# Making masks, triangle and scales on chip instead of loading them, in a gated linear attention followed by a maxout network

## The chip, the core and the metric

The kernel runs on one core of a Trainium2 chip. A core has five engines with a queue of their own each: PE (TensorE, matrix products; its weight loads are shown as PEld), DVE (VectorE), ACT (ScalarE), POOL (GpSimd) and SP (SyncE, which here issues all transfers). Each engine works through its instructions strictly in program order, and waits on semaphores where an instruction needs a result of another engine or of a transfer. The metric is the time of one execution on the device in microseconds; lower is better. The kernel before took 141.66 us (median of three runs, 141.11 to 141.95).

## What is computed

```python
for t in range(S):                       # q, k, v, alpha: (4, 8, 768, 48)
    state = alpha[:, :, t, :, None] * state + np.einsum('bhd,bhe->bhde', k[:, :, t], v[:, :, t])
    y[:, :, t] = np.einsum('bhd,bhde->bhe', q[:, :, t], state)
x = y.transpose(0, 2, 1, 3).reshape(B * S, H * D)          # (3072, 384)
h = np.maximum(np.maximum(x @ w1, x @ w2), x @ w3)         # w1, w2, w3: (384, 768)
out = h @ w_out                                            # w_out: (768, 384)
```

Inputs and output are float32; inside, most products are of float16 operands.

## The kernel before

The recurrence is done in 12 steps. Step s handles 256 tokens of batch s mod 4, so steps 0 to 3 are the first third of the sequence of the four batches, and a step needs the state that step s - 4 left. The 256 tokens are two units of 128 tokens, and within a unit two neighbouring tokens share a partition (R = 2). For each step four loads of 384 KB bring alpha, q, k and v (`load`, one letter of "akqv" for the tile: ra, rk, rq, rv) into rings of four buffers, as rows of 384 bytes.

Then, for a step: alpha of a pair is multiplied (`pair_decay`, m), its logarithm taken (`logs`, N, `inverse`, r), and PE sums the logarithms along the sequence with a triangular matrix `upto` and a 4-column matrix `pick` (`sums`, c). Exponentials of these sums are the decays (`decay_in` e, `decay_out` f, `totals` g), by which DVE or POOL scale k and q (`near_k` u, `near_q` w, `scale_k` k, `scale_q` q). v is scaled by a column constant `vs_c` (V). PE turns q and k with the identity `ident` (T, kept by t), or, from step 5 on, a transfer turns them (D). PE forms the scores (A, line L304), DVE multiplies them by the causal mask `pmask`, or by `rowmask`, spread from it, for step 0 (`masked`, a), PE applies them to v and applies q to the state (Y, L330), and the result is kept as xT (x). The new state is formed by S, s, z and y, with gates M.

The network uses max(a, b, c) = a + max(0, b - a, c - a) with the maximum kept in hT: `differ` (d, L418) makes w2 - w1 and w3 - w1 as `wdif`; the w1 part goes straight to the output as x (w1 w_out), a product that is formed once from a halved w1 (`halve` b, turned by B, kept by n) and w_out (C, P, p). For each step six gate products G of six matmuls (L452) are reduced by `maxed` (h), and two or more output products O (L486) of nine matmuls are scaled by `ys_c` (o) and stored (W). Weight tiles K0 to K8 are column blocks of w1, w2, w3 (K3 is block 1 of w1), K9 to K11 pairs of row blocks of w_out. K0 to K7 are first loaded into the ring buffers that steps 2 and 3 will use for alpha, q, k and v, so for instance `l0@2` (alpha of step 2) can be issued only when K0 has been read by d0, d1 and b0.

The order of everything is a string, `ORDER`. A piece such as `k0v@1` is: letter, index, engine (v DVE, p POOL, a ACT), step; `#` names the PSUM banks. Nothing reorders it: each engine gets its pieces in this order. `H` pieces are warm matmuls on a zeroed tile, which compute nothing; `H2^k0@1` also waits for a named piece. Before the order, `clear_padding` zeroes padding columns: DVE the 16 half states and two la tiles, POOL the vu, qk and vt tiles.

The constants `upto`, `pick`, `vs_c`, `ys_c`, `undo_c` come as one array `ca` (34.5 KB), and `ident` and `pmask` as `cb` (64 KB), both computed on the host, and loaded by the pieces J1 and J0 between the first loads:

```python
        l0@0 J1@0 l1@0 J0@0 l3@0 l0@1 r0a@0 m0v@0 l2@0 N0a@0 r1a@0 u0v@0 H15@0#0 c0@0#0 g0a@0 e0a@0 K0@0 f0a@0
```

Of the kernel before, what the change touches and what calls it, by code (L numbers as in the profile page):

```python
# [10 lines left out]
FP16 = mybir.dt.float16  # L11

# [11 lines left out]
def kernel(  # L24
# [39 lines left out]
    rr = np.arange(P)  # L64
    tri_np = (
        ((rr[:, None] > MID) & (rr[:, None] <= rr[None, :])).astype(np.float16)
        - ((rr[:, None] <= MID) & (rr[:, None] > rr[None, :])).astype(np.float16)
    )
    w2_np = np.stack([rr <= MID, rr > MID], 1).astype(np.float16)
    ur, jr = rr // J, rr % J  # L70
    same = (ur[:, None] == ur[None, :]).astype(np.float16)
    upto_np = same * np.tile(tri_np[R - 1::R, R - 1::R], (U, U))
    pick_np = np.zeros((P, U, 2), np.float16)
    for u in range(U):
        pick_np[u * J:(u + 1) * J, u] = w2_np[::R]
    token = np.concatenate([R * np.arange(J) + r for r in range(R)])
    pmask_np = (token[:, None] <= token[None, :]).astype(np.float16)
    at_pair = LAM * (R * jr + R - 1 - MID)
    at_token = LAM * (rr // R * R + R - 1 - MID)
    c32_np = np.stack(  # L80
        [np.exp(at_pair + SIGMA), np.exp(-at_token - SIGMA), 0 * rr - LAM * P / 2], 1
    ).astype(np.float32)
    ca_np = np.concatenate([np.concatenate([upto_np, pick_np.reshape(P, -1)], 1).view(np.float32), c32_np], 1)
    cb_np = np.concatenate([np.eye(P, dtype=np.float16), pmask_np], 1)

# [28 lines left out]
    def load_weight(_, i, eng):  # L114
        home = staged(i)
        if i < 9:
            w = (moe_w1, moe_w2, moe_w3)[i % 3]
            queues[eng].dma_start(home.rearrange("p (f j) -> p f j", f=NF),
                                  w.rearrange("(f p) j -> p f j", p=P)[:, :, i // 3 * 2 * P:(i // 3 + 1) * 2 * P])
        else:  # L120
            queues[eng].dma_start(home.rearrange("p (j m) -> p j m", j=2),
                                  moe_w_out.rearrange("(j p) m -> p j m", p=P)[:, 2 * (i - 9):2 * (i - 8)])

    ca = cpool.tile([P, P // 2 + U + 3], FP32, name="ca")
    cb = cpool.tile([P, 2 * P], FP16, name="cb")
    rowmask = cpool.tile([P, R, P], FP16, name="rowmask")

    def load_const(_, i, eng):
        c, c_np = ((ca, ca_np), (cb, cb_np))[i]
        queues[eng].dma_start(c, nc.inline_tensor(c_np, name=f"c{i}").ap())  # L130

    half = ca.bitcast(FP16)
    upto, pick = half[:, :P], half[:, P:P + 2 * U]
    c32 = ca[:, P // 2 + U:]
    ident, pmask = cb[:, :P], cb[:, P:2 * P]
    vs_c, ys_c, undo_c = c32[:, 0:1], c32[:, 1:2], c32[:, 2:3]
# [6 lines left out]
    sts = [[cpool.tile([P, HP, 2, D], FP16, name=f"st{b}_{i}") for i in range(2)] for b in range(B)]  # L143

    def clear_padding():
        for st in (st for pair in sts for st in pair):
            for i in range(2):
                nc.vector.memset(st[64 * i:64 * (i + 1), :, 1 - i], 0.0)
        for la in las:
            nc.vector.memset(la.rearrange("p r a b c -> p (r a b) c")[:, :, D:], 0.0)  # L150
        for vu in vus:
            nc.gpsimd.memset(vu.rearrange("p u a b c -> p (u a b) c")[:, :, D:], 0.0)
        for qk, vt in zip(qks, vts):
            nc.gpsimd.memset(qk.rearrange("p r i a b c -> p (r i a b) c")[:, :, D:], 0.0)
            nc.gpsimd.memset(vt.rearrange("p a b c -> p (a b) c")[:, :, D:], 0.0)


# [69 lines left out]
    def sums(s, *_):  # L227
# [4 lines left out]
        for p in range(HP):  # L232
            for n, (r, _) in enumerate(parts):
                nc.tensor.matmul(lps(s, 1)[:, H * D + 2 * U * p:H * D + 2 * U * (p + 1)],
                                 las[s % 2][:, r, p].rearrange("p a b -> p (a b)"), pick,
# [71 lines left out]
    def spread_mask(_, i, eng):  # L307
        for u in range(U):
            for r in range(R):
                copy(eng, rowmask[u * J:(u + 1) * J, r], pmask[r * J:(r + 1) * J])  # L310

    def masked(s, x, eng):
# [5 lines left out]
        else:  # L318
            nc.vector.tensor_mul(lats[s % 2][u][:, i], bank(("aps", s, u, i), [HP, P]),  # L319
                                 pmask.unsqueeze(1).broadcast_to([P, HP, P]))  # L320
# [95 lines left out]
    def differ(_, i, eng):  # L416
        jg, g = divmod(i, 2)
        engines[eng].tensor_sub(  # L418
            wdif[:, :, g, column_group(jg)], staged(3 * jg + 1 + g).rearrange("p (f j) -> p f j", f=NF),
            staged(3 * jg).rearrange("p (f j) -> p f j", f=NF))  # L420

    def halve(_, i, eng):
        copy(eng, w1h[i], staged(3 * i).rearrange("p (f j) -> p f j", f=NF))
# [98 lines left out]
    def warm_after(n, name):  # L522
# [5 lines left out]
        "l": load_step, "J": lambda _, i, eng: load_const(0, 1 - i, eng), "I": spread_mask, "K": load_weight, "H": warm,  # L528
# [9 lines left out]
    def emit(order):  # L538
# [12 lines left out]
        l0@0 J1@0 l1@0 J0@0 l3@0 l0@1 r0a@0 m0v@0 l2@0 N0a@0 r1a@0 u0v@0 H15@0#0 c0@0#0 g0a@0 e0a@0 K0@0 f0a@0  # L551
        k0v@0 l1@1 V0v@0 K2@0 H6@0#1 H1^k0@0#1 S0@0#1,2 K1@0 l2@1 I0a@0 r0a@1 m0p@1 l3@1 M0p@0 N0a@1 w0v@0 q0v@0
        H6@0#3 c0@1#3 l0@4 f0a@1 H1@0#4 T1@0#4 s0v@0 z0v@0 b0v@0 e0a@1 t1a@0 u0v@1 k0v@1 H1@0#5 B0@0#5 T0@0#6
        y0a@0 r1a@1 d1v@0 t0a@0 d0v@0 g0a@1 n0a@0 H1@0#7 H2^k0@1#7 H0^d1@0#7 A1@0#7,0 A0@0#1,4 w0v@1 l0@2 a2v@0
        K3@0 q0p@1 V0a@1 K4@0 a0v@0 K5@0 s1v@0 a3v@0 l1@2 H3@0#6 H2^a2@0#6 S0@1#6,3 s0a@1 m0p@4 a1v@0 v1a@1
        T1@1#5 T0@1#7 t1a@1 M0p@1 z0v@1 y0p@1 l2@2 Y0@0#1,2 t0v@1 x0v@0 K6@0 v0a@1 H2@0#0 A0@1#0,6 A1@1#4,5
        m0v@2 Y3@0 N0a@2 a0v@1 x1a@0 a3v@1 H1@0#7 c0@2#7 r0a@2 g0a@2 G0@0#1 d2v@0 N0a@4 c0@4#0 K7@0 s1v@1 b1a@0
        G2@0#2 K8@0 d3v@0 e0a@4 e0a@2 a2v@1 h2a@0 l3@2 G3@0#5 g0a@4 a1v@1 l0@3 f0a@2 B1@0#3 r1a@2 u0p@2 k0v@2
        Y2@1#4 Y3@1 x1a@1 Y0@1#2 K11@0 K9@0 G1@0#6 w0v@2 q0v@2 x0a@1 r0a@4 G2@1#7 n1a@0 G0@1#4 h2a@1 T0@2#2
        h0v@0 h3v@0 h0a@1 d4p@0 T1@2#3 f0a@4 h1v@0 t1a@2 t0v@2 G1@1#7 l1@4 G3@1#1 d5p@0 h3v@1 r1a@4 K10@0  # L560
        A1@2#5,4 V0a@2 l0@5 G4@0#0 a3v@2 a2v@2 A0@2#6,3 b2a@0 S0@2#2,1 M0p@4 M0p@2 G5@1#4 s0v@2 m0p@3 v1a@2
        a1v@2 l2@4 G4@1#5 a0v@2 z0p@2 h4a@0 v0v@2 y0a@2 G5@0#2 h1v@1 Y2@2#3 Y0@2#6 x0v@2 N0a@3 Y3@2 B2@0#0 l1@3
# [73 lines left out]
```

## Time and profile before

| | |
|---|---|
| three runs, median (range) | 141.66 us (141.11 to 141.95) |
| the profiled execution, its own time | 143.14 us |
| the profiled execution, span from first to last instruction | 141.4 us |
| moved by transfers | 32.42 MB, mean 229 GB/s |
| mean granted PE clock | 0.997 |

A group line of the profile reads: line, engine, operation, output <- inputs, shape, count | busy time, mean ns of one | idle time just before, and what ended it. A line of the timeline reads: start and duration in us, engine (SPq: transfer issue), line, operation, count, and in brackets idle time before it and what ended it. "PE bank L452 x6" in the chain of waits means six matmuls of line 452 on the path that ended last. Several pieces go through helpers, so that one line (L164, `copy`) stands for many pieces; the tile names tell them apart.

### The profile page before, as it was taken

How to read it: one execution, taken by the hardware profiler on the slowest of the kernel's cores; microseconds unless marked ns; L12 is line 12 of the kernel's file. 1: busy time of each engine (PE TensorE's matmuls, PEld its weight loads, DVE VectorE, ACT ScalarE, POOL GpSimd, SP SyncE). 2: the span in 40 equal slices, each digit the busy share in tenths (PEclk: the TensorE clock that was granted, in tenths of full speed). 3: DMA queues.
4: the chain of work that ended last, by engine and by line, in shares of the span. 5: the costliest groups of instructions: out<-in, count | busy, mean ns of one | idle time of the engine just before them, and what ended most of it. 6: DMA issues, size and time to landing. Idle time of an engine off the chain costs nothing.

```text
span 141.4 us, 5309 instructions
## 1 busy us (share of the span) xinstructions
PE 130.9 (93%) x2238; PEld 94.6 (67%) x2238; DVE 116.7 (83%) x220; ACT 96.0 (68%) x202; POOL 65.4 (46%) x102
## 2 busy tenths in 40 slices
PE   6977697999998999999998999999999999999990
PEld 2434265787865676688767867787567876788670
DVE  5559979998999998979797987979989899847511
ACT  3667689999974978999997734497657480554121
POOL 8230171268080059939892999458507501700000
PEclk9999999999999999999999999999999999999998
DMA  4999999999996299998999899999999859401433
GB/s 111 273 333 349 298 261 335 321 326 365 302 282 173 52 322 320 278 308 151 230 216 228 250 188 291 272 169 233 197 267 318 182 112 257 154 5 63 159 111 111
DMA packets 73031, 32.42 MB, mean 229 GB/s; under 512 B 65456, under 2 KB 73008, under 8 KB 73008
## 3 DMA queue, kind: packets, MB, share of 16 engines
q1 hardware_dynamic: 73008, 32.09, 88.3%
q8 instruction: 17, 0.28, 0.7%
q14 instruction: 6, 0.05, 0.1%
HBM read 23.69 MB, written 4.72 MB: 201 GB/s over the span
## 4 chain that ended last, share of the span: by engine, by line
PE 51%; DMA 16%; DVE 16%; SPq 6%; POOL 3%; ACT 3%; issue 2%; DVEq 0%
PE bank L452 22%; PE bank L486 17%; DMA ra<-in_alpha_dram 5%; PE bank L330 5%; DMA rv<-in_v_dram 4%; DMA qkT<-qk 4%; DMA rq<-in_q_dram 3%; SPq L102 3%; PE bank L304 3%; DVE lat L319 2%; PE bank L283 2%; DVE qk L260 2%; DVE hT L461 2%; SPq L290 2%; PE bank L388 2%
## 5 line engine op out<-in xcount | busy, mean ns | idle before, releaser
L452 PE MATMUL bank<-xT,wdif 128*128 128x256 f16 x432 | 51.5, 273 | 0.3 <-DVE wdif L418 0.3
L452 PEld LDWEIGHTS <-wdif 128*128 128x128 f16 x432 | 40.7, 98 | 6.5 <-DVE wdif L418 0.6
L319 DVE TENSOR_TENSOR lat<-bank,cb 128x512 f16<-128x512 f32 x44 | 27.8, 682 | 1.5 <-PE bank L304 1.5
L486 PE MATMUL bank<-wo,hT 128*128 128x384 f16 (+1 forms) x150 | 27.5, 320 | 0.0
L461 DVE TENSOR_TENSOR hT<-bank,h 128x512 f16<-128x512 f32 x36 | 23.8, 686 | 3.9 <-PE bank L452 2.1
L486 PEld LDWEIGHTS <-hT 128*128 128x128 f16 x150 | 14.5, 98 | 9.0
L465 ACT ACTIVATE h<-bank 128x512 f16<-128x512 f32 x20 | 11.7, 601 | 7.9 <-PE bank L452 7.9
L486 PE MATMUL bank<-w1o,xT 128*128 128x384 f16 (+1 forms) x75 | 15.9, 320 | 0.0
L168 ACT ACTIVATE ob<-bank,ca 128x384 f32<-128x384 f32 (+1 forms) x15 | 8.4, 572 | 10.8 <-PE bank L486 8.0
L205 POOL TENSOR_TENSOR ra<-ra 128x384 f32<-128x384 f32 x9 | 9.0, 999 | 11.1 <-DMA ra<-in_alpha_dram 10.8
L505 PE MATMUL bank<-hT 128*128 128x512 f16 x41 | 12.2, 420 | 1.2 <-DVE hT L603 1.2
L463 DVE TENSOR_SCALAR h<-bank 128x512 f16<-128x512 f32 x16 | 10.7, 685 | 3.1 <-PE bank L452 3.0
L162 ACT CAST st<-kept 64x192 f16<-64x192 f32 x28 | 9.7, 347 | 4.9 <-POOL kept L404 4.7
L164 POOL COPY vu<-vt 64x384 f16<-64x384 f16 x16 | 8.0, 502 | 9.6 <-DVE vt L170 8.9
L162 ACT COPY vu<-vt 64x384 f16<-64x384 f16 x24 | 12.2, 509 | 0.4
L260 POOL TENSOR_TENSOR qk<-rq,ac 128x768 f16<-128x768 f32 x5 | 9.1, 1816 | 7.2 <-DVE rq L222 7.1
L260 POOL TENSOR_TENSOR qk<-rk,ic 128x768 f16<-128x768 f32 x5 | 9.4, 1877 | 2.3 <-DVE rk L219 1.6
L162 ACT CAST xT<-bank 128x384 f16<-128x384 f32 x14 | 6.3, 479 | 5.7 <-PE bank L330 5.7
L222 POOL TENSOR_TENSOR rq<-rq,ic 128x384 f32<-128x384 f32 x6 | 6.0, 1002 | 7.7 <-ACT ic L216 7.7
L304 PE MATMUL bank<-qkT 48*64 48x128 f16 x384 | 8.6, 219 | 0.7 <-DMA qkT<-qk 0.4
L170 DVE TENSOR_SCALAR ob<-bank,ca 128x384 f32<-128x384 f32 (+1 forms) x10 | 5.8, 591 | 3.8 <-PE bank L486 3.8
L168 ACT ACTIVATE vt<-rv,ca 128x768 f16<-128x768 f32 x8 | 7.5, 935 | 2.0 <-DMA rv<-in_v_dram 1.9
(82 smaller groups left out, 214.3 us busy)
## 6 DMA issues: line engine op xcount, KB each, us to landing
ra<-in_alpha_dram SPq DMA_DIRECT2D x12, 384.0 KB, 5.3
rk<-in_k_dram SPq DMA_DIRECT2D x12, 384.0 KB, 5.2
rv<-in_v_dram SPq DMA_DIRECT2D x12, 384.0 KB, 5.6
rq<-in_q_dram SPq DMA_DIRECT2D x12, 384.0 KB, 4.8
out_dram<-ob SPq DMA_DIRECT2D x23, 192.0 KB, 2.2
wst<-in_moe_w_out_dram SPq DMA_DIRECT2D x3, 384.0 KB, 6.1
ra<-in_moe_w_dram SPq DMA_DIRECT2D x2, 384.0 KB, 5.2
rk<-in_moe_w_dram SPq DMA_DIRECT2D x2, 384.0 KB, 6.2
```

The source lines that it names most:

```text
L162: nc.scalar.copy(out=dst, in_=src)
L168: nc.scalar.mul(dst, src, col)
L205: engines[eng].tensor_mul(raw("a", s, 0), raw("a", s, 0), raw("a", s, 1))
L260: engines[eng].tensor_mul(dst, src, by)
L304: nc.tensor.matmul(aps[i][to * J:(to + 1) * J, a * U + n, :], qkT[rows, r, 1, p, cols], qkT[rows, :, 0, p, cols], start=True, stop=True)
L319: nc.vector.tensor_mul(lats[s % 2][u][:, i], bank(("aps", s, u, i), [HP, P]), pmask.unsqueeze(1).broadcast_to([P, HP, P]))
L452: nc.tensor.matmul(gps[:, j, :], wdif[:, f, g, jj * P:(jj + 1) * P], xT[:, f].rearrange("p u t -> p (u t)"), start=(f == 0), stop=(f == NF ...
L461: nc.vector.tensor_max(hTs[s % NH][:, 2 * jg:2 * jg + 2, :], gps, h)
L463: nc.vector.tensor_scalar_max(h, gps, 0.0)
L465: nc.scalar.activation(out=h, in_=gps, func=AFT.Relu)
L486: nc.tensor.matmul(ops, lhs, (w1o if what == "x" else wo16)[:, j, cols], start=((what, j) == every[0]), stop=((what, j) == every[-1]))
L505: nc.tensor.matmul(wps, blank[:, :P], blank, start=True, stop=True)
```

## The change

The two constant arrays and their loads go. Their contents are made on chip: POOL makes a column of partition numbers (`iota`), a tile of ones, and from it by affine selections the triangle `upto`, the identity and `pmask`; DVE makes `pick` by memsets, and the scales from the partition numbers by bitwise operations and multiply-add, on which ACT takes one exponential of 128x2. The states become one tile `spread`, cleared by two memsets instead of 16. The padding of the vu tiles and of two of the four vt tiles moves from POOL to ACT. w_out is loaded with two neighbouring rows in one partition (rows of 3 KB instead of two of 1.5 KB), which renumbers the hidden channels; `differ` and `halve` therefore write their columns with a stride of 128 elements. And the order string is a new one, made by a search for the kernel with these changes.

```diff
-    ca = cpool.tile([P, P // 2 + U + 3], FP32, name="ca")
-    cb = cpool.tile([P, 2 * P], FP16, name="cb")
-        queues[eng].dma_start(c, nc.inline_tensor(c_np, name=f"c{i}").ap())
...
-                                  moe_w_out.rearrange("(j p) m -> p j m", p=P)[:, 2 * (i - 9):2 * (i - 8)])
+                                  moe_w_out.rearrange("(g p j) m -> g p j m", p=P, j=2)[i - 9])
...
+    def make_sums():
+        nc.gpsimd.iota(place_of, [[0, 1]], base=0, channel_multiplier=1)
+        nc.gpsimd.memset(ones, 1.0)
+        nc.gpsimd.affine_select(upto, ones, [[1, P]], AOP.is_ge, 0.0, base=0, channel_multiplier=-1)
+        nc.gpsimd.memset(upto[:J, J:], 0.0)
+        for u in range(U):
+            block = upto[u * J:u * J + J // 2, u * J:(u + 1) * J]
+            nc.gpsimd.tensor_scalar_add(block, block, -1.0)
+
+    def make_scales():
+        nc.vector.memset(pick, 0.0)
+        for u in range(U):
+            for i in range(2):
+                nc.vector.memset(pick[u * J + i * J // 2:u * J + (i + 1) * J // 2, u, i:i + 1], 1.0)
+        nc.vector.memset(undo_c, -LAM * P / 2)
+        at = LAM * (R - 1 - MID)
+        nc.vector.tensor_single_scalar(place_in[:, 0:1], place_of, J - 1, AOP.bitwise_and)
+        nc.vector.tensor_single_scalar(place_in[:, 1:2], place_of, P - R, AOP.bitwise_and)
+        nc.vector.tensor_scalar(vs_c, place_in[:, 0:1], R * LAM, at + SIGMA, AOP.mult, AOP.add)
+        nc.vector.tensor_scalar(ys_c, place_in[:, 1:2], -LAM, -at - SIGMA, AOP.mult, AOP.add)
+        nc.scalar.activation(out=c32[:, 0:2], in_=c32[:, 0:2], func=AFT.Exp)
+
+    def make_masks():
+        nc.gpsimd.affine_select(ident, ones, [[1, P]], AOP.is_equal, 0.0, base=0, channel_multiplier=-1)
+        for r in range(R):
+            rows = slice(r * J, (r + 1) * J)
+            nc.gpsimd.affine_select(pmask[rows], ones[rows].rearrange("p (r j) -> p r j", r=R),
+                                    [[r, R], [1, J]], AOP.is_ge, 0.0, base=-r, channel_multiplier=-1)
...
+    spread = cpool.tile([P, 2, B, HP, 2, D], FP16, name="spread")
+    sts = [[spread[:, i, b] for i in range(2)] for b in range(B)]
     def clear_padding():
-        for st in (st for pair in sts for st in pair):
-            for i in range(2):
-                nc.vector.memset(st[64 * i:64 * (i + 1), :, 1 - i], 0.0)
+        nc.vector.memset(blank, 0.0)
         for la in las:
             nc.vector.memset(la.rearrange("p r a b c -> p (r a b) c")[:, :, D:], 0.0)
+        zeros = blank[:, :HP * U * 2 * (64 - D)].rearrange("p (a c) -> p a c", c=64 - D)
         for vu in vus:
-            nc.gpsimd.memset(vu.rearrange("p u a b c -> p (u a b) c")[:, :, D:], 0.0)
-        for qk, vt in zip(qks, vts):
+            nc.scalar.copy(out=vu.rearrange("p u a b c -> p (u a b) c")[:, :, D:], in_=zeros)
+        for vt in vts[2:]:
+            nc.scalar.copy(out=vt.rearrange("p a b c -> p (a b) c")[:, :, D:], in_=zeros)
+        for i, (qk, vt) in enumerate(zip(qks, vts)):
             nc.gpsimd.memset(qk.rearrange("p r i a b c -> p (r i a b) c")[:, :, D:], 0.0)
-            nc.gpsimd.memset(vt.rearrange("p a b c -> p (a b) c")[:, :, D:], 0.0)
+            if i < 2:
+                nc.gpsimd.memset(vt.rearrange("p a b c -> p (a b) c")[:, :, D:], 0.0)
+
+    def clear_states():
+        for i in range(2):
+            nc.vector.memset(spread[64 * i:64 * (i + 1)].rearrange("p x b a i d -> p (x b a) i d")[:, :, 1 - i], 0.0)
...
     def differ(_, i, eng):
         jg, g = divmod(i, 2)
         engines[eng].tensor_sub(
-            wdif[:, :, g, column_group(jg)], staged(3 * jg + 1 + g).rearrange("p (f j) -> p f j", f=NF),
-            staged(3 * jg).rearrange("p (f j) -> p f j", f=NF))
+            wdif[:, :, g, column_group(jg)].rearrange("p f (j n) -> p f n j", j=2), staged(3 * jg + 1 + g).rearrange("p (f n j) -> p f n j", f=NF, j=2),
+            staged(3 * jg).rearrange("p (f n j) -> p f n j", f=NF, j=2))
     def halve(_, i, eng):
-        copy(eng, w1h[i], staged(3 * i).rearrange("p (f j) -> p f j", f=NF))
+        copy(eng, w1h[i].rearrange("p f (j n) -> p f n j", j=2), staged(3 * i).rearrange("p (f n j) -> p f n j", f=NF, j=2))
...
     ORDER = """
+        K3@0 b1v@0 H8@0#0 B1@0#0 l0@1 m0v@1 r0a@1 r1a@1 l0@0 l2@1 w0v@1 l1@1 l2@0 N0a@1 H4@0#1 c0@1#1 r0a@0
+        f0a@1 e0a@1 r1a@0 m0p@0 N0a@0 H6@0#2 c0@0#2 f0a@0 l1@0 e0a@0 l3@1 K0@0 K1@0 q0v@1 K2@0 d1p@0 u0v@1 k0v@1
+        H4@0#3 T0@1#3 t0a@1 K5@0 w0v@0 T1@1#4 l3@0 u0v@0 q0v@0 l0@4 k0v@0 t1v@1 V0a@1 g0a@0 H2@0#5 H3^t0@1#5
+        S0@1#5,6 s0v@1 g0a@1 M0v@1 z0v@1 d3p@0 M0p@0 v0a@1 I0a@0 d0v@0 s1v@1 T0@0#7 A1@1#3,4 a2v@1 A0@1#2,5
+        b0a@0 H2@0#1 H1^d0@0#1 B0@0#1 K4@0 a1v@1 a3v@1 l0@2 l1@2 T1@0#6 t1v@0 l2@2 t0v@0 H1@0#3 H3^a3@1#3
+        A1@0#3,5 K6@0 a0v@1 y0a@1 v1a@1 m0p@4 V0a@0 n0v@0 r0a@4 S0@0#4,6 s0a@0 Y2@1#7 A0@0#2,1 a2v@0 Y3@1 x1a@1
+        a0v@0 K7@0 Y0@1#4 x0v@1 H1@0#3 H0^x1@1#3 G0@1#3 a1v@0 K8@0 z0p@0 d2v@0 y0p@0 G1@1#7 Y3@0#2 G2@1#4 r0a@2
...
     with tc.manual_schedule():
-        nc.vector.memset(blank, 0.0)
+        make_sums()
+        make_masks()
         clear_padding()
+        make_scales()
+        clear_states()
         emit(ORDER)
```

Over the whole order the pieces that compute are the same ones, except that J0 and J1 are gone; many changed their engine (for instance d1 and d3 from DVE to POOL). The counts on PE are unchanged but for the warm matmuls: 45 before, 39 after. As before, steps 0 to 4 are turned on PE and steps 5 to 11 by transfers.

## The prediction

> **What bounds the kernel now.** I read the page first (shares, then the slices), then the chain of waits, then the timeline.
>
> ```profile
> span 141.4 us, 5309 instructions
> PE 130.9 (93%) x2238; PEld 94.6 (67%) x2238; DVE 116.7 (83%) x220; ACT 96.0 (68%) x202; POOL 65.4 (46%) x102
> ...
> PE   6977697999998999999998999999999999999990
> ...
> DMA  4999999999996299998999899999999859401433
> GB/s 111 273 333 349 298 261 335 321 326 365 302 282 173 52 322 320 278 308 151 230 216 228 250 188 291 272 169 233 197 267 318 182 112 257 154 5 63 159 111 111
> ```
>
> PE is busy in nearly every slice, so it looks like the bound. But the first slices hold warm matmuls and waits, and the transfers run at nine tenths from the second slice on. The timeline (start, duration, what, and in brackets what ended the wait) shows where useful PE work becomes dense:
>
> ```profile
> 0.74 0.45 SPq L102 DMA_DIRECT2D ra<-in_alpha_dram  x1
> ...
> 1.09 3.08 DVE L148 MEMSET st<- 64x96 uint32 x16
> ...
> 1.26 0.56 SPq L130 DMA_DIRECT2D ca<-c  x1
> ...
> 2.33 0.92 SPq L130 DMA_DIRECT2D cb<-c  x1
> ...
> 4.10 0.31 POOL L155 MEMSET vt<- 128x256 f16 x1
> ...
> 4.34 0.52 ACT L214 ACTIVATE ic<-ra 128x384 f32<-128x384 f32 x1 [2.33 <-DMA ra<-in_alpha_dram]
> ...
> 8.90 1.00 POOL L205 TENSOR_TENSOR ra<-ra 128x384 f32<-128x384 f32 x1 [4.49 <-DMA ra<-in_alpha_dram]
> ...
> 10.07 0.56 DVE L222 TENSOR_TENSOR rq<-rq,ic 128x384 f32<-128x384 f32 x1 [1.64 <-DMA rq<-in_q_dram]
> ...
> 19.42 1.00 POOL L205 TENSOR_TENSOR ra<-ra 128x384 f32<-128x384 f32 x1 [0.44 <-DMA ra<-in_alpha_dram]
> ...
> 23.48 0.82 PE L452 MATMUL bank<-xT,wdif 128*128 128x256 f16 x6
> ...
> 29.90 1.06 PE L283 MATMUL bank<-cb,qk 128*128 128x128 f16 x16
> ...
> 42.98 1.14 PE L440 MATMUL bank<-wo,w1T 128*128 128x384 f16 x6 [0.70 <-DVE h L463]
> ...
> 43.95 0.33 PE L231 MATMUL bank<-la,ca 128*128 128x384 f16 x1
> ...
> 75.93 0.42 PE L304 MATMUL bank<-qkT 48*64 48x128 f16 x16 [0.39 <-DMA qkT<-qk]
> ```
>
> The first gate product starts at 23.48, and the product of the weights is done at 43.95. Between them DVE sets the pace, after them PE:
>
> ```profile
> 0.00:23.40 23.40, 18.29 (x302) 9.55 (x303) 17.04 (x44) 15.81 (x32) 8.70 (x22) 1.00 0.97 277
> 23.40:44.00 20.60, 19.40 (x310) 15.10 (x307) 19.85 (x33) 18.15 (x38) 9.48 (x9) 1.00 1.08 318
> 44.00:138.00 94.00, 93.19 (x1633) 69.99 (x1631) 79.58 (x145) 61.66 (x134) 47.21 (x71) 1.00 0.85 202
> ```
>
> (Columns: stretch, its length, busy us of PE, PE loads, DVE, ACT, POOL, granted clock, share and GB/s of the transfers.) From 23.4 to 44.0 DVE is busy 19.85 of 20.60; from 44 to 138 PE 93.19 of 94.00. So there is next to nothing to gain after 44, short of a PE wait or two; what can move is when the state reached at 44 is reached. I therefore follow DVE and the loads up to that state.
>
> **The change part by part.** *Loads.* Two loads of 34.5 and 64 KB go, 0.56 and 0.92 us of issue, and 98.5 of 384 KB, 0.26 of a load. From 4.34 (first load used) to 10.07 (fifth) are four loads and the constants: 5.73 / 4.26 = 1.35 us a load; from there to 19.42 (twelfth) 9.35 / 7 = 1.34. That includes times at which issues waited; at the 318 GB/s of the second stretch a load (0.393 MB) would take 1.24, and at the 349 of the fourth slice 1.13. I take 1.25, with 1.13 and 1.34 as bounds.
>
> The new order loads K3 first, then alpha of steps 1 and 0, and q of step 1 as fourth: 4.34 + 3 x 1.25 = 8.1, k of step 1 at 9.35, q and k of step 0 at 10.6 and 11.85, K0 and K1 at 14.35 and 15.6. Step 1 comes before step 0 now.
>
> *Constants.* No row shows an iota or a selection. Nearest on POOL: a 128x4 operation of two inputs, 0.20, and one of 128x384, 1.00:
>
> ```profile
> L205 POOL TENSOR_TENSOR ra<-ra 128x384 f32<-128x384 f32 x9 | 9.0, 999 | 11.1 <-DMA ra<-in_alpha_dram 10.8 <-DVE lat L319 0.4
> L377 POOL TENSOR_TENSOR gm<-ge 128x4 f32<-128x4 f32 x9 | 1.7, 199 | 0.0
> L154 POOL MEMSET qk<- 128x512 f16 x4 | 2.1, 528 | 0.0
> L162 ACT COPY rowmask<-cb 64x128 f16<-64x128 f16 x4 | 1.2, 294 | 0.0
> L603 DVE MEMSET hT<- 128x256 uint32 x1 | 0.3, 272 | 0.9 <-PEq L620 0.9
> L162 ACT COPY vu<-vt 64x384 f16<-64x384 f16 x24 | 12.2, 509 | 0.4
> ```
>
> A selection of 128x128 lies between 0.2 and 1.0; 0.4, nearer the small one, as it has a third of the elements and one input. POOL then has about 2.6 us of constants and, as four qk and two vt memsets, 2.4 of padding: from 0.73 to 5.7 (4.6 to 8.2 at the bounds). Its first real work waits for alpha of step 0 at 6.8. DVE pays two memsets of 768 words, 0.8 each by three times 0.272, for sixteen that took 3.08, and ten tiny ones for the scales, about 0.15 each: free at 4.5, as K3 lands. ACT pays five padding copies of 128x256, which I put at 0.4 (between 0.29 and 0.51, the two rows), and a small exponential: free at about 4.5, before its alpha at 5.6. All of that is hidden by the first loads; the rival below says what if not. Each of these waits holds a queue: DVE's scales wait for the iota, and behind them stand the state memsets and b1; ACT's exponential holds the logarithms.
>
> *DVE up to the first gate.* From q of step 1 on, DVE runs through these without a long wait (durations from the groups):
>
> ```profile
> L260 DVE TENSOR_TENSOR qk<-rq,ac 128x768 f16<-128x768 f32 x7 | 6.7, 956 | 0.2
> L222 DVE TENSOR_TENSOR rq<-rq,ic 128x384 f32<-128x384 f32 x6 | 3.3, 554 | 2.0 <-DMA rq<-in_q_dram 2.0
> L319 DVE TENSOR_TENSOR lat<-bank,cb 128x512 f16<-128x512 f32 x44 | 27.8, 682 | 1.5 <-PE bank L304 1.5
> L164 DVE COPY qkT<-bank 128x1024 f16<-128x1024 f16 x3 | 2.0, 680 | 0.0
> L400 DVE TENSOR_TENSOR fb<-bank,kept 128x192 f32<-128x192 f32 x8 | 2.7, 349 | 0.8 <-POOL kept L404 0.8
> L164 DVE CAST xT<-bank 128x384 f16<-128x384 f32 x10 | 5.3, 552 | 0.2
> L164 DVE CAST w1o<-bank 128x384 f16<-128x384 f32 x1 | 0.5, 549 | 0.0
> L418 POOL TENSOR_TENSOR wdif<-rv,rk 128x768 f16<-128x768 f32 x1 | 1.8, 1849 | 2.3 <-DMA rv<-in_moe_w_dram 2.3
> L404 DVE TENSOR_TENSOR kept<-fb,gm 128x192 f32<-128x192 f32 x3 | 2.7, 889 | 0.0
> L404 DVE TENSOR_TENSOR kept<-fa,gm 128x192 f32<-128x192 f32 x5 | 1.8, 351 | 1.0 <-POOL gm L377 0.9
> ```
>
> w, u of two steps: 4 x 0.555; q, k of two steps: 4 x 0.955; three qkT copies 2.04; s, z, s 1.05; a gate 0.2 (as POOL's); d0 0.96, of the shape of q and k; six lat 6 x 0.65 (0.682 with some overlap); n0 0.55; x0 0.55. Sum 15.3. From 8.1 that is 23.4, and 0.15 until k of step 0 lands at 11.85: the first gate at **23.5**, against 23.48 before (23.0 and 24.0 with loads 1.13 and 1.34 apart). K3 in front costs all other data one load, and DVE gains what it did with b0 and d1 (0.55 and 0.96) in the chain before: b1 is done while it had nothing to do, d1 and d3 go to POOL, 1.85 each, from K2 (16.9) to 20.6, before y0 of step 0 is wanted.
>
> *DVE from there to the product of the weights.* In order: a, d2, m, a, u, s, n, h, q, k, which is 6.9 (before, 6.4 passed from the first gate to the same turn, at 29.90); then eleven lat and h at 0.68, t, n, z, s, x, and C, q, C: 11.3. PE in the same time does 17 gate products, where it did 16 before, and reaches the weights' product at 23.5 + 17.55 and ends its 18 matmuls, 0.162 each, at 44.0. Before, it ended at 43.95. One gate product more is done:
>
> ```profile
> 47.52 1.46 PE bank L486 x9
> ...
> 49.43 0.65 PE bank L452 x6
> ```
>
> So **-0.65**. *After 44* the same pieces remain on PE, which sets the pace. The wait for the turned q and k of step 6 at 75.93 may go: before, A of step 6 followed Y of step 5 at once; now an output product (1.46) and a gate product (0.65) stand between. In exchange two stores stand ahead of those transfers in SP's queue: between 0 and -0.4, I take -0.2. The tail, twelve gates and five products, is the same on PE. The 3 KB rows change three loads of 48; nothing waits for them in my count: 0.
>
> Stride: the six differences and three halvings write with a stride of 128 elements. The trace has a strided read (xT, 0.552) as fast as an unstrided one (w1o, 0.549), and no strided write; bounds are no cost and twice the time; I take none, as the arithmetic is one element a cycle either way.
>
> Sum: -0.85 on 141.4 of span, 140.55. The profiled execution itself took 143.14, 1.74 beyond its span; the three runs lie at 141.66, 1.5 below that one. I put the difference on the median: **140.8**.
>
> **The rivals.** *POOL's start-up, slower.* Before, POOL idles from 4.41 to 8.90 ahead of its first operation that isn't a memset, and starts it as its load lands: whatever it needed to get ready for such an operation, up to 4.5 us, was hidden. Now the iota stands first, at 0.73. With a start-up of L, DVE's m of step 1 ends at about 4.2 + L instead of 6.1: it decides from L = 2, and at 4.5 the chain of q starts 1.8 later: 142.6. Against it: the landing of the load alone explains the start at 8.90, so L may as well be nothing. The Trainium skill (GPSIMD Engine Reference, section 2.1 Instruction dispatch) puts the first call to a freshly loaded kernel of POOL at about 6 us. By that figure an estimate of the shift is 3.3 and of the time 144.1; the row speaks against it, as 6 us from 4.41 would have ended at 10.4, after the start at 8.90.
>
> *Strided writes at twice the time, slower.* d0 and d2 add 1.9 on DVE's chain; d1 and d3 add 3.7 on POOL, so y0 of step 0 comes 1.9 after PE wants it: 142.7.
>
> *POOL and DVE hold each other up, slower.* kept takes 0.889 where POOL works beside it, 0.351 else. With d1, d3 and other work moved to POOL, three such cases more on DVE's chain: +1.6, 142.4.
>
> *No change.* Loads at 1.34 and the wait at 75.9 stays: 23.48 against 24.0, 141.5.
>
> *Faster still.* Loads at 1.13 (-0.5) and PE's waits after 44, 0.8 by the windows, gone too: 139.6.
>
> **How the numbers follow.** The forecast 0.36, own range 140.2 to 141.4; faster still 0.17; no change 0.11; start-up 0.12; stride 0.11; POOL beside DVE 0.13. A measurement tells about 0.5% (0.7 us) from no change: 140.95 to 142.37. The forecast lies mostly below (0.23 of 0.36), with 0.17 makes 0.40; the rest of it, no change and a little of the last make 0.25; 0.35 slower. The range, 139.4 to 143.3, takes in the rivals on both sides; what lies outside is half of faster still and the worse part of the three slower ones.
>
> **What would show it.** Right: the first gate at 23 to 24, 17 gate products before 44, DVE without long idle from 8. Wrong: iota long after 0.75 with DVE waiting for it; wdif on DVE above 1.0 or on POOL above 2.0; PE below 93 of 94 after 44, which would be an order whose later waits I didn't see.

## The result, and the profile after

The changed kernel takes 159.21 us (median of 4 runs, 157.75 to 159.53), the kernel before, run beside it, 141.78 (141.11 to 141.95). The ratio is 1.1219, with an interval of 1.1141 to 1.1298: 17.4 us slower, where 140.8 was predicted with 143.3 as the upper end. Some executions of a kernel are 1 to 5% longer than the others; the medians below take in all runs, the ratios leave such runs out, and the profiles of the kernel before and of e12 are of such longer executions.

The head of the page of the changed kernel, with the rows of the slices that differ most from before:

```profile
span 157.5 us, 5319 instructions
...
PE 136.5 (87%) x2232; PEld 98.8 (63%) x2232; DVE 127.2 (81%) x211; ACT 100.4 (64%) x208; POOL 84.9 (54%) x111
...
PE   6299703966699999999999999999999999989990
...
PEclk9999995796559999999999999999999999999998
DMA  4999900993991979679769999799699676601405
```

The loss is at the front: PE has slices of 2, 0 and 3 tenths in the first 28 us, and the granted clock is low in slices 7 and 8 and in 10 to 12. From the 13th slice on PE is as full as before. POOL has 19.5 us more of busy time with nine instructions more, and DVE 10.5 us more with nine fewer.

The timeline of the changed kernel (start, duration, what, wait before it). First the constants made on chip:

```profile
0.91 0.13 POOL L115 IOTA place_of<- 128x1 int32 x1 [0.39 <-POOLq L634]
...
1.25 0.29 POOL L117 TENSOR_SCALAR_AFFINE_SELECT upto<-ones 128x128 f16<-128x128 f16 x1
...
3.32 0.70 DVE L167 MEMSET spread<- 64x768 uint32 x1 [0.20 <-issue]
...
3.63 0.20 ACT L134 ACTIVATE c<-c 128x2 f32<-128x2 f32 x1
...
4.20 3.55 DVE L175 CAST ob<-rv 128x768 f16<-128x768 f32 x1 [0.18 <-DMA rv<-in_moe_w_dram]
...
4.97 0.99 POOL L161 MEMSET qk<- 128x512 f16 x2
...
7.81 0.82 PE L440 MATMUL bank<-ident,ob 128*128 128x128 f16 x6 [2.96 <-DVE ob L175]
...
8.09 0.55 DVE L233 TENSOR_TENSOR rq<-rq,ic 128x384 f32<-128x384 f32 x1
```

POOL starts at 0.91, DVE is free at 4.02, ACT at 3.83, POOL at 5.96. But the halving b1, which begins at 4.20, takes 3.55 where 0.55 was counted, and PE waits 2.96 for it. Then, on the same view, the differences:

```profile
16.27 3.67 POOL L429 TENSOR_TENSOR wdif<-rk,ra 128x768 f16<-128x768 f32 x1 [8.53 <-DMA rk<-in_moe_w_dram]
17.35 2.10 DVE L388 TENSOR_TENSOR gm<-ge 128x4 f32<-128x4 f32 x1
...
19.04 3.59 ACT L173 CAST ob<-ra 128x768 f16<-128x768 f32 x1
19.54 3.80 POOL L429 TENSOR_TENSOR wdif<-rq,rv 128x768 f16<-128x768 f32 x1
19.76 6.47 DVE L429 TENSOR_TENSOR wdif<-rq,ra 128x768 f16<-128x768 f32 x1
22.93 2.87 POOL L388 TENSOR_TENSOR gm<-ge 128x4 f32<-128x4 f32 x1
26.29 0.20 PE L535 MATMUL bank<-wdif,hT 128*128 128x48 f16 x1 [7.60 <-DVE wdif L429]
...
32.62 1.47 PE L463 MATMUL bank<-xT,wdif 128*128 128x256 f16 x12 [0.22 <-DVE xT L175]
...
33.08 3.55 DVE L429 TENSOR_TENSOR wdif<-ra,rv 128x768 f16<-128x768 f32 x1
33.28 3.71 POOL L233 TENSOR_TENSOR rq<-rq,ic 128x384 f32<-128x384 f32 x1 [0.79 <-ACT ic L227]
...
37.93 2.86 DVE L230 TENSOR_TENSOR rk<-rk,ra 128x384 f32<-128x384 f32 x1
```

Two things are to be seen. Every operation that writes with the new pattern takes 3.55 to 3.9, on DVE, ACT and POOL alike, save one. That one, a difference on DVE beside one on POOL, takes 6.47, and operations that do not write so are long too when they run beside one that does: a product of 128x4 takes 2.10 on DVE and 2.87 on POOL (0.20 before on POOL), a product of 128x384 3.71 on POOL and 2.86 on DVE (1.00 and 0.55 before). The first gate product starts at 32.62 instead of 23.48; that alone is 9.1 of the 17.4 us. In the list of PE's waits (what was waited for, us in all, times, longest) the new pattern stands at the top three times:

```profile
PE bank L535 <- DVE wdif L429: 7.6, 1, 7.6
PE bank L440 <- DVE ob L175: 3.0, 1, 3.0
PE bank L463 <- DVE wdif L429: 2.3, 1, 2.3
```

### The profile page after: what moved, and what is told of

The parts are those of the page before. It is cut to its first block, busy times and chain, and to the rows that moved or that the text cites. A ratio compares the mean times of both kernels' runs of the same rounds, so it can differ in the third digit from the quotient of the medians.

```text
span 157.5 us, 5319 instructions
## 1 busy us (share of the span) xinstructions
PE 136.5 (87%) x2232; PEld 98.8 (63%) x2232; DVE 127.2 (81%) x211; ACT 100.4 (64%) x208; POOL 84.9 (54%) x111
## 4 chain that ended last, share of the span: by engine, by line
PE 70%; DVE 18%; DMA 5%; issue 2%; ACT 1%; SPq 0%; DVEq 0%
PE bank L463 29%; PE bank L497 19%; DVE wdif L429 6%; PE bank L516 5%; PE bank L341 4%; PE bank L315 3%; DVE lat L330 3%; PE bank L294 3%; DMA out_dram<-ob 3%; PE bank L399 2%; DVE ob L175 2%; DMA rv<-in_moe_w_dram 2%; PE bank L451 2%; DVE lat L326 2%; PE bank L242 1%
## 5 line engine op out<-in xcount | busy, mean ns | idle before, releaser
L463 PE MATMUL bank<-xT,wdif 128*128 128x256 f16 x432 | 54.2, 280 | 4.9 <-DVE wdif L429 2.3
L330 DVE TENSOR_TENSOR lat<-bank,pmask 128x512 f16<-128x512 f32 x44 | 27.7, 680 | 1.0 <-PE bank L315 0.8
L472 DVE TENSOR_TENSOR hT<-bank,h 128x512 f16<-128x512 f32 x36 | 23.5, 683 | 6.0 <-PE bank L463 4.1
L497 PEld LDWEIGHTS <-hT 128*128 128x128 f16 x150 | 14.5, 98 | 8.9
L179 ACT ACTIVATE ob<-bank,c 128x384 f32<-128x384 f32 (+1 forms) x18 | 10.0, 571 | 15.2 <-PE bank L497 8.1
L271 POOL TENSOR_TENSOR qk<-rq,ac 128x768 f16<-128x768 f32 x6 | 10.9, 1816 | 6.2 <-DVE rq L233 3.8
L516 PEld LDWEIGHTS <-hT 128*128 128x128 f16 x35 | 3.8, 125 | 14.1 <-issue 12.2
L415 POOL TENSOR_TENSOR kept<-fa,gm 128x192 f32<-128x192 f32 x9 | 4.6, 506 | 12.6 <-DVE fa L411 7.8
L220 ACT ACTIVATE la<-ra 128x384 f16<-128x384 f32 x12 | 6.3, 521 | 7.4 <-DVE ra L216 7.1
L474 DVE TENSOR_SCALAR h<-bank 128x512 f16<-128x512 f32 x12 | 8.1, 683 | 3.5 <-PE bank L463 3.4
L173 ACT CAST spread<-kept 64x192 f16<-64x192 f32 x24 | 8.7, 362 | 2.0 <-POOL kept L415 1.0
L179 ACT ACTIVATE vt<-rv,c 128x768 f16<-128x768 f32 x10 | 9.3, 934 | 0.0
L497 PEld LDWEIGHTS <-xT 128*128 128x128 f16 x75 | 6.6, 98 | 3.4
```

The lines of the kernel that those rows point to most:

```text
L173: nc.scalar.copy(out=dst, in_=src)
L179: nc.scalar.mul(dst, src, col)
L271: engines[eng].tensor_mul(dst, src, by)
L463: nc.tensor.matmul(gps[:, j, :], wdif[:, f, g, jj * P:(jj + 1) * P], xT[:, f].rearrange("p u t -> p (u t)"), start=(f == 0), stop=(f == NF ...
L472: nc.vector.tensor_max(hTs[s % NH][:, 2 * jg:2 * jg + 2, :], gps, h)
L474: nc.vector.tensor_scalar_max(h, gps, 0.0)
```

## The experiments

Two suspects stood from the start: the stride of the writes, and the searched order. The half clock came third. In the table, "first gate" is the start of the first gate product in the profiled execution, "by 44" counts gates (six products each) begun before 44 us, and "last" is the start of the last matmul. Ratios are against the kernel before, run on the same chip in the same stretch of time; the medians come from four such stretches, in which the kernel before took 141.78 to 142.89, so that a difference of two medians can be off by about 1 us.

| kernel | us (median) | ratio, interval | first gate | by 44 | last |
|---|---|---|---|---|---|
| before | 141.78 | 1 | 23.48 | 16.0 | 137.68 |
| after | 159.21 | 1.1219 (1.1141 to 1.1298) | 32.62 | 5.0 | 153.70 |
| e1: after, whole writes, 1.5 KB rows | 144.88 | 1.0161 (1.0097 to 1.0225) | 23.06 | 17.0 | 139.78 |
| e2: after, whole writes, 3 KB rows | 143.88 | 1.0105 (1.0065 to 1.0145) | 22.77 | 18.0 | 137.88 |
| e3: before with the new writes | 162.65 (one run) | | 31.96 | 4.8 | 157.19 |
| e4: before with constants on chip | 141.93 | 0.9976 (0.9936 to 1.0016) | 23.04 | 16.7 | 136.92 |
| e6: after, waits filled with matmuls | 158.86 | 1.1144 (1.1060 to 1.1227) | 32.23 | 6.0 | 153.00 |
| e7: after, halvings whole | 151.32 | 1.0610 (1.0551 to 1.0670) | 25.00 | 11.5 | 145.44 |
| e10: after, differences whole | 151.07 | 1.0664 (1.0587 to 1.0741) | 29.06 | 9.8 | 145.44 |
| e11: e2 with sums later | 144.61 | 1.0211 (1.0145 to 1.0277) | 22.78 | 17.3 | 138.51 |
| e8: e4 with 3 KB rows, whole writes | 141.24 | 0.9897 (0.9848 to 0.9945) | 22.86 | 17.0 | 136.04 |
| e12: e8 again | 142.79 | 1.0004 (0.9950 to 1.0058) | 22.86 | 16.0 | 138.53 |

### Rows and writes as before, order and constants as after (e1)

```diff
-   wdif[:, :, g, column_group(jg)].rearrange("p f (j n) -> p f n j", j=2), staged(...).rearrange("p (f n j) -> p f n j", ...)
+   wdif[:, :, g, column_group(jg)], staged(...).rearrange("p (f j) -> p f j", f=NF)
-   copy(eng, w1h[i].rearrange("p f (j n) -> p f n j", j=2), staged(3 * i).rearrange("p (f n j) -> p f n j", ...))
+   copy(eng, w1h[i], staged(3 * i).rearrange("p (f j) -> p f j", f=NF))
-   moe_w_out.rearrange("(g p j) m -> g p j m", p=P, j=2)[i - 9]
+   moe_w_out.rearrange("(j p) m -> p j m", p=P)[:, 2 * (i - 9):2 * (i - 8)]
```

> The changed kernel, but w_out is loaded as before (rows of 1.5 KB) and the differences and halvings write whole rows again; new order and constants on chip stay. Theory S (the writes with a stride of 128 elements cost all of it): the differences come back to 0.96 us on DVE and 1.85 on POOL, the halvings to 0.55 and 0.82, PE's first gate to 23 to 24 us, the time to 139.5 to 142. Rival O (the new order and the constants are slow by themselves, the stride adds some): the time stays above 145.

144.88, between the two ranges given: above the 142 of theory S, just below the 145 of its rival. 14.3 of the 17.4 us are gone (15.0 by the ratios), and the first gate is at 23.06. What stays, 1.6%, is the order or the constants.

### 3 KB rows kept, the step put on the read instead of the write (e2)

```diff
-   wdif[...].rearrange("p f (j n) -> p f n j", j=2), staged(...).rearrange("p (f n j) -> p f n j", f=NF, j=2)
+   wdif[...].rearrange("p f (j n) -> p f j n", j=2), staged(...).rearrange("p (f n j) -> p f j n", f=NF, j=2)
```

The same elements go to the same places (the halvings alike); only the order in which they are written changes.

> The changed kernel with its 3 KB rows, but the differences and halvings write whole rows and read with a stride of 2 float32 elements instead. S, as a matter of writes: within 0.7 us of the kernel with whole rows, differences at 0.96 and 1.85 again. S, as a matter of any scattered access of two bytes or four: differences stay above 2 us and the time above 148.

143.88, where within 0.7 us of e1 was expected: 1.0 below. The list of the differences in this kernel (duration in ns least, median, most; first and last start):

```profile
L429 DVE TENSOR_TENSOR wdif<-rq,ra x1: 951/951/951, 15.1 to 15.1; 128x768 f16<-128x768 f32 x1
L429 POOL TENSOR_TENSOR wdif<-rk,ra x1: 2164/2164/2164, 16.2 to 16.2; 128x768 f16<-128x768 f32 x1
L429 POOL TENSOR_TENSOR wdif<-rq,rv x1: 2169/2169/2169, 18.3 to 18.3; 128x768 f16<-128x768 f32 x1
```

The order in which an operation walks over its output is worth 15.3 us here (159.21 to 143.88; 15.8 by the ratios). The read with a step costs DVE nothing in a difference (0.951 against 0.952 to 0.959 before), 0.4 in a halving (0.95 against 0.55), and POOL 0.3 in a difference (2.17 against 1.85).

### The new writes alone, in the kernel before (e3)

The edit of the diff in `differ`, `halve` and the rows of w_out, with the order and the loaded constants of before.

> The kernel before with nothing but the 3 KB rows and the writes with a stride of 128 elements. Theory S: each difference 3.6 us on either engine, each halving 3.6, so that DVE's chain to the weights' product (four differences and one halving on DVE) grows by 4 x 2.6 + 3.0 = 13.4 and the time comes to 150 to 156. Rival O: at most 3 us over before, 145.

162.65 in a single run, 20 us above before and more than the 150 to 156 expected. That sum had counted the longer operations and not what they hold up beside them: on DVE a product of 0.96 takes 2.25 and one of 0.56 takes 3.46 beside the two differences on POOL. Whether this is the whole gap, and why the writes cost more in this order than in the new one, was not followed up.

### The constants alone (e4)

Before's order without J0 and J1, and the new `make_sums`, `make_scales`, `make_masks`, `clear_padding`, `clear_states`.

```diff
-   l0@0 J1@0 l1@0 J0@0 l3@0 l0@1 r0a@0 ...
+   l0@0 l1@0 l3@0 l0@1 r0a@0 ...
```

> The order of before without the two constant loads, constants made on chip as in the change, whole rows. If the constants on chip are hidden by the first loads (prediction): 140.5 to 142, within 0.7 us of before, with alpha, k and v of step 0 landing up to 0.4 earlier. If they hold up a queue: the first gate later than 23.5 by what they hold, time above 142.5.

0.9976, and the interval (0.9936 to 1.0016) takes in 1: making the constants on chip costs no more than 0.2%, and what it may bring is no more than 0.6%.

### What a write pattern costs by itself (e5)

One engine at a time casts 768 float32 of each partition to float16, with different write patterns; the core of it:

```python
for step in (1, 2, 4, 8, 16):
    cast(eng, dst[:, :N * step].rearrange("p (n s) -> p n s", s=step)[:, :, 0], src)
for step in (2, 4):      # float32 written
    cast(eng, wide.bitcast(FP32)[:, :N * step].rearrange("p (n s) -> p n s", s=step)[:, :, 0], src)
for run in (2, 4, 8):
    cast(eng, wide[:, :N * 2].rearrange("p (n r) -> p n r", r=2 * run)[:, :, :run], src.rearrange(...))
cast(eng, wide[:, :N].rearrange("p (f j n) -> p f n j", f=3, j=2), src.rearrange("p (f n j) -> p f n j", f=3, j=2))
cast(eng, wide[:, :N].rearrange("p (j n) -> p n j", j=2), src.rearrange("p (n j) -> p n j", j=2))
```

> The kernel's work is left out; it stores zeros. Each of DVE, ACT and POOL in turn casts the same 768 float32 per partition to float16 with eleven write patterns. If single 2-byte writes away from their neighbour are what costs (some 4.6 ns each in the changed kernel), the unbroken write takes about 0.55 (DVE), 0.8 (ACT), 1.0 (POOL), every step of 2, 4, 8, 16 elements takes about 3.6 on all three, 4-byte elements in steps take less, and runs of 2, 4, 8 elements come down to about 1.8, 0.9 and the unbroken time. If it is instead the alternation between two places 256 bytes apart, the plain steps stay within 1.3 us and only the last two patterns (alternating halves) take 3.6. If the cost grows with the distance, step 16 takes several times step 2.

The timeline of POOL in that kernel (steps of 1, 2, 4, 8, 16 float16, then of 2 and 4 float32, then runs of two float16, then the changed kernel's pattern):

```profile
50.10 0.82 POOL L52 CAST pstep<-srcp 128x768 f16<-128x768 f32 x1 [49.66 <-ACTq L99]
50.86 1.03 POOL L52 CAST wide<-srcp 128x768 f16<-128x768 f32 x1
51.96 1.89 POOL L52 CAST wide<-srcp 128x768 f16<-128x768 f32 x1
53.91 3.58 POOL L52 CAST wide<-srcp 128x768 f16<-128x768 f32 x1
57.56 3.38 POOL L52 CAST wide<-srcp 128x768 f16<-128x768 f32 x1
61.01 0.87 POOL L52 COPY wide<-srcp 128x768 f32<-128x768 f32 x1
61.93 1.54 POOL L52 COPY wide<-srcp 128x768 f32<-128x768 f32 x1
63.54 0.83 POOL L52 CAST wide<-srcp 128x768 f16<-128x768 f32 x1
...
66.21 3.56 POOL L52 CAST wide<-srcp 128x768 f16<-128x768 f32 x1
```

The first two theories miss, and the third holds in part: steps of 4, 8 and 16 bytes take 1.03, 1.89 and 3.58, but from there the cost stays (3.38 at 32 bytes). Two neighbours together cost as little as the unbroken write (0.83). It fits a count of the 16-byte pieces that are entered: 192, 384 and 768 of them, so (3.58 - 1.89) / 384 = 4.4 ns for each piece that is entered with 2-byte elements standing alone; with 4-byte elements (1.54 - 0.87) / 384 = 1.7 ns. Two neighbours are not charged in this way: they enter 192 pieces too, and take 0.83 where single elements take 1.03. The changed kernel's pattern enters a new piece with every element, as it goes to and fro between two places 256 bytes apart, and pays like a step of 16 bytes. ACT gives the same numbers within 0.02. DVE pays half for plain steps, and for the changed kernel's pattern the whole:

```profile
13.48 1.87 DVE L52 CAST wide<-srcv 128x768 f16<-128x768 f32 x1
15.38 1.84 DVE L52 CAST wide<-srcv 128x768 f16<-128x768 f32 x1
...
20.52 3.53 DVE L52 CAST wide<-srcv 128x768 f16<-128x768 f32 x1
24.09 1.87 DVE L52 CAST wide<-srcv 128x768 f16<-128x768 f32 x1
```

(Steps of 8 and 16; then the pattern in three blocks; then the same to and fro in one block of 384 pairs.) Why a 2-byte element costs more than a 4-byte one these runs do not show.

### The half clock taken away (e6)

```diff
-   b0a@0 H2@0#1 H1^d0@0#1 B0@0#1 ...
+   b0a@0 H36@0#1 H1^d0@0#1 B0@0#1 ...
-   ... y0p@0 G1@1#7 Y3@0#2 ...
+   ... y0p@0 H11@0#7 G1@1#7 Y3@0#2 ...
```

> The changed kernel, with 34 more blank matmuls ahead of the wait for the first difference and 11 ahead of the second pair of gates (their products are used by nothing). If the half clock after the long waits of PE costs what the windows suggest (20.8 us at 0.75 granted, PE 16.7 busy), this gives 3 to 5 us back: 154 to 156, granted clock above 0.97. If the loss is the waits for the strided writes alone, it stays at 158 to 160 with a higher granted clock.

158.86, ratio 1.1144, whose interval overlaps that of the changed kernel: no gain that can be told. Stretches of this kernel, then of the changed one (columns as in the prediction):

```profile
34.00:55.00 21.00, 17.36 (x321) 13.65 (x320) 19.51 (x26) 15.43 (x28) 16.00 (x13) 1.00 0.80 233
```

```profile
34.00:55.00 21.00, 16.91 (x289) 13.20 (x289) 18.50 (x24) 14.97 (x26) 15.80 (x13) 0.76 0.75 223
```

The clock went from 0.76 to 1.00 and the last matmul from 153.70 to 153.00. So the low clock follows from the waits, and it is not what makes the kernel long. That it costs nothing is not shown: with the full clock PE begins a run of five gates at 51.22 instead of 53.10, 1.9 us earlier, and loses the lead at 58.16, where it waits 1.91 for DVE's copies of w_out. One of them took 2.16 there, beside a product on POOL, and 0.55 in the changed kernel:

```profile
55.94 2.16 DVE L175 CAST wo<-wst 128x768 f16<-128x768 f32 x1
```

### The halvings and the differences apart (e7 and e10)

e7 writes only the halvings whole, e10 only the differences, each by the edit of e2.

> The changed kernel with the three halvings writing unbroken (they read with a step of 2 instead) and the six differences writing scattered as before. Three halvings of 3.55 to 3.62 become 0.9 to 1.0, some 8 us of engine time in all, of which the first (2.96 us of PE waiting) stands ahead of the first transposition but not ahead of the first gate, which the differences set. If the differences carry nearly all the loss: 155 to 158. If the halvings carry a share like their engine time (10.8 of 35.8 us): 153 to 155.

> The changed kernel with the six differences writing unbroken (they read with a step of 2) and the three halvings writing singly as before: the other half of the split. With both whole it took 143.9, with the halvings whole 151.3, with neither 159.2. If the two parts add up: 151 to 152. If the halvings' loss came only because they stood in line behind the differences: 145 to 148.

151.32 and 151.07. e7 lies below both ranges given for it: three halvings are worth 7.9 us. Six differences are worth 8.1, of the 14.2 by which they are longer (25.0 in all against 10.9 in e2); four of them run on POOL, two on DVE. Together 16.0, against 15.3 for both at once, so the two parts add up (8.6 and 7.9 by the ratios, against 15.8).

The 7.9 is also the time by which the three halvings are longer (3.55, 3.59 and 3.62 against about 0.95 each), but that is chance. In e10, where only the halvings are slow, the first gate comes 6.3 us later than in e2 (29.06 against 22.77). The first halving accounts for 2.6 to 2.7 of that: DVE reaches its first product of q and decay at 11.31 instead of 8.60. Two small operations of DVE account for another 3.0: they now run beside POOL's differences, and take 1.26 and 2.27 where they took 0.15 and 0.36 in e2, ahead of those differences:

```profile
17.26 1.26 DVE L388 TENSOR_TENSOR gm<-ge 128x4 f32<-128x4 f32 x1
...
18.55 2.27 DVE L415 TENSOR_TENSOR kept<-fa,gm 128x192 f32<-128x192 f32 x1
```

The halving was expected not to stand ahead of the first gate; it does, by way of PE's sums and ACT's exponentials, which wait behind its transposition in PE's order.

### Who holds up whom (e9)

After a meeting of the three engines one writes 768 elements singly, and another works beside it.

> The kernel's work is left out; it stores zeros. After a meeting point of the three engines one of them writes 768 float16 singly (the changed kernel's pattern, 3.55 alone), while a second (a) writes singly too, (b) writes unbroken, (c) does four casts of four elements. Theory from the trace of the changed kernel, where a difference took 6.47 on DVE beside one of 3.80 on POOL and a 128x4 product 2.10 instead of 0.16: the write port is shared, and DVE and POOL writing singly together take some 7 in all, and the tiny operations beside a single-writing engine 1 to 3 instead of 0.1 to 0.2. Rival: the neighbours were held up by something else (another engine, reads); then DVE and POOL end together at 3.6 to 4.0 and the tiny operations keep 0.1 to 0.2.

The timeline of that kernel (vo is written by DVE, ao by ACT, po by POOL):

```profile
13.04 3.53 DVE L52 CAST vo<-srcv 128x768 f16<-128x768 f32 x1
...
13.30 3.57 POOL L52 CAST po<-srcp 128x768 f16<-128x768 f32 x1
...
24.52 3.57 POOL L52 CAST po<-srcp 128x768 f16<-128x768 f32 x1
24.58 3.92 DVE L52 CAST vo<-srcv 128x768 f16<-128x768 f32 x1
28.64 0.57 DVE L52 CAST vo<-srcv 128x768 f16<-128x768 f32 x1
28.76 3.57 ACT L50 CAST ao<-srca 128x768 f16<-128x768 f32 x1
...
36.16 3.57 POOL L52 CAST po<-srcp 128x768 f16<-128x768 f32 x1
...
36.23 3.53 DVE L52 COPY vtiny<-vtiny 128x4 f32<-128x4 f32 x1
```

Half of the theory falls. DVE and POOL, both writing singly, run side by side in 3.53 and 3.57: the writes are not shared out. But an unbroken cast that DVE begins just after POOL takes 3.92 instead of 0.57, and a copy of four elements 3.53, where the same copy beside ACT takes 0.16: these two get nothing until POOL is nearly done. Beside ACT neither is longer. So it behaves as a lock between DVE and POOL that some operations need and others do not, held for as long as the holder runs. The Trainium skill (SBUF — State Buffer, section Who interferes with whom) says so: DVE's second port pair is POOL's, an exclusive lock for the whole instruction, needed by DVE's two-port modes and, against a POOL operation that reads SBUF, by its operations with two inputs in SBUF. The traces agree: the difference on DVE of 6.47 began 0.22 after one on POOL that ended at 23.34, and ended 2.89 after that, somewhat less than its own 3.55, as DVE is let in a little before POOL's end; the 128x4 products wait in the same way. An operation with one input in PSUM is not held: DVE's product of a bank and `rowmask` that begins at 37.33, beside POOL's difference from 36.95 to 40.87, takes its usual 0.68. The lock was to be seen in the kernel before, where one of the products called kept took 1.97 beside a POOL product of 2.13 that had begun at 39.98, and 0.35 elsewhere:

```profile
40.36 1.97 DVE L404 TENSOR_TENSOR kept<-fb,gm 128x192 f32<-128x192 f32 x1
```

### The order (e11, e8 and e12)

e11 moves one early sum of e2's order, for which PE waited 0.77 us:

```diff
-   ... N0a@5 c0@5#2 l1@5 V0a@4 f0a@5 g0a@5 M0p@3 l0@8 h1v@2 h5v@2 O0@0#4 t0v@4 S0@4#3,1 ...
+   ... N0a@5 l1@5 V0a@4 M0p@3 l0@8 h1v@2 h5v@2 O0@0#4 t0v@4 c0@5#2 f0a@5 g0a@5 S0@4#3,1 ...
```

> The changed kernel with 3 KB rows, strided reads and unbroken writes (143.9), its order altered at one place: the sums of step 5 (which kept PE waiting 0.77 us for ACT's logarithm at 44.5) and the two exponentials behind them are moved behind the first projection and the turn of step 4. If such waits of PE behind an early sum are what the new order costs, the last matmul comes 0.5 to 1.0 earlier (137.0 to 137.4 from the start) and the time falls to 143.0 to 143.4. If the order's cost is spread over many places, the wait moves to the next instruction and the last matmul stays at 137.6 to 138.2.

144.61 and a last matmul at 138.51: nothing came of it, and both are even later than the rival had it. e8 and e12 are one kernel: e4 with the rows and the reads of e2.

> The order of before without the two constant loads, constants made on chip, w_out in 3 KB rows, differences and halvings writing unbroken and reading with a step of 2. If the new order is what costs the 1.0 to 1.6% left without the scattered writes: 141.5 to 142.3 (0.994 to 1.001), as the constants alone. If 3 KB rows and strided reads cost by themselves: 143 to 144. If the longer rows bring what their name suggests: 140.5 to 141.3.

> The order of before, constants on chip, 3 KB rows with strided reads, a second time. If it is faster than before: a ratio of 0.985 to 0.995 again. If the first result was chance: 0.996 to 1.003, as with the constants alone.

0.9897 the first time and 1.0004 the second, so a gain is not settled; but by both it is below the 1.0105 and 1.0211 of the same parts in the new order. Where the new order loses shows in the stretch from 45 to 60, first e2, then e8:

```profile
45.00:60.00 15.00, 13.34 (x274) 9.56 (x274) 12.80 (x25) 13.01 (x29) 9.94 (x14) 1.00 0.93 242
```

```profile
45.00:60.00 15.00, 15.00 (x333) 10.72 (x331) 14.34 (x29) 13.12 (x28) 9.64 (x13) 1.00 0.95 260
```

In the order of before PE is busy all of these 15 us (15.00 in e4 too; 14.84 in e12 and in the kernel before). In the new one 1.6 us go (13.39 in e11), in waits that shift when a piece is moved: of 1.1 and 0.8 in e2, of 0.8, 0.5 and 0.3 in e11. Which pieces would have to move to win them back stays open.

## Why the prediction was wrong, step by step

- *Loads.* Right: q of step 1, issued at 2.46, lands 5.5 later, at 7.96, where 8.1 was worked out. That DVE's first product with it begins at 8.09 is partly luck: DVE comes to it straight from the work that the slow halving had put off, and in e2, where it was free, it waited until 7.94 for ACT's exponential.
- *Constants hidden by the first loads.* Right. A selection takes 0.29 (0.4 taken), POOL is free at 5.96 (5.7), DVE at 4.02 (4.5), ACT at 3.83 (4.5), and e4 shows no cost that can be told.
- *DVE's sum to the first gate, 23.5.* Right but for the writes: 32.62 with them, 22.77 and 23.06 without (e2, e1; the range was 23.0 to 24.0). The 9.85 us between 32.62 and 22.77 can be read off DVE's rows against e2: the halving 2.6 longer, the 128x4 product 1.95 longer (2.10 against 0.15), the difference 5.5 longer (6.47 against 0.95), some 10 in all. Of that 1.95 and 2.9 are waits for POOL's differences, so about half of the delay is the writes themselves and half the lock.
- *17 gates before the weights' product.* By 44, 5 with the new writes, 18 and 17 without.
- *Stride: "bounds are no cost and twice the time; I take none, as the arithmetic is one element a cycle either way".* This is the step that failed: a term that was put at nothing. The arithmetic does not set the time; the writes do, by e5 at 4.4 ns for each 16-byte piece entered. Against 0.55 for a halving and 0.95 for a difference on DVE, it was 6.5 and 3.7 times; on POOL about twice (3.67 against 1.85), which alone lay near the bound. The strided read quoted as the nearest row says nothing of a strided write. The term is worth 15.3 of the 17.4 us by e2, what the lock adds to it included.
- *The rival "strided writes at twice the time, 142.7"* had the mechanism, not the size, and named only differences; the halvings, which it left out, are half of the loss (e7).
- *The rival "POOL and DVE hold each other up"* is real too, as a lock. Its price follows the operation on the other side, and so grew with the writes. The prediction priced it too low from its own row: 0.889 is the mean of three, of which two took 0.35 and one, beside a product of 2.13 on POOL, 1.97; a single such case cost 1.6, the sum that was put down for three.
- *The rival of POOL's start-up* is refuted: the iota stands at 0.91 and takes 0.13, the selection after it starts at 1.25. The Trainium skill's figure of about 6 us (GPSIMD Engine Reference, section 2.1 Instruction dispatch) does not show here.
- *After 44 the same pieces remain on PE.* Wrong by 1.6 us between 45 and 60, apart from the writes (e2 and e11 against e8 and e4). The wait for the turned q and k of step 6 is gone, as expected, but others came. With whole writes the new order is not 0.6% faster but 1.0 to 1.6% slower.
- *3 KB rows, 0.* Not settled: e2 against e1 and e8 against e4 point to 0.6 and 0.8% in their favour, e12 to none.

Of the signs listed, "wdif on DVE above 1.0 or on POOL above 2.0" was named as what would show it wrong, and that is the row that did. "PE below 93 of 94 after 44" came true only without the new writes: 91.78 in e2, 93.44 in the changed kernel, whose loss lies ahead of it.

## What to carry to other kernels

When a permutation must sit on one side of an operation that narrows to 16 bits, put the step on the read and let the write run through; a transfer in longer rows is not worth a scattered write behind it. A strided read is no row for a strided write: where the trace shows no operation of the kind, the upper bound belongs at several times, the more so where nine operations share it. And look at what runs beside a long POOL operation: DVE's small operations with all inputs in SBUF were held for most of it here, those on a PSUM bank not. A group mean can hide such a wait; the single rows show it.

## What the runs showed of the hardware

- Single 2-byte writes cost 4.4 ns for each 16-byte piece that is entered, on ACT and POOL, and 2.2 on DVE for plain steps ((1.87 - 1.02) / 384, from steps of 8 and 4), 4-byte writes 1.7 on POOL; with gaps as long as the runs, two neighbouring elements are enough to write at full speed (0.83).
- DVE needs as long as the others (3.53) where the pattern has three blocks, and 1.87 where it has one.
- Two engines that write singly do not slow each other down, but the lock between DVE and POOL turns a copy of four elements (0.16) into 3.53.
- A granted clock of 0.76 over 21 us cost at most a small part of the time: at 1.00 PE was 1.9 us ahead at 51, and its last matmul came 0.7 earlier.
